# Weight splits of three experts issued in other phases of the expert loop

## The chip, the cores and the metric

The kernel runs on one core of one Trainium2 chip. The metric is the device time of one execution in microseconds (us), as the median of repeated runs. The core has five engines with a queue of instructions each: TensorE (PE, with its weight loads shown as PEld), VectorE (DVE), ScalarE (ACT), GpSimd (POOL) and SyncE (SP), which here issues most of the transfers between memory and the core's own storage.

## The reference, cut to what matters

Chunked attention gives 1536 tokens of 512 features. A gate sends each token to one of eight experts (two matrices, 512x1024 and 1024x512, with a ReLU between them); then a dense layer pair follows for all tokens (512x2048 and 2048x512).

```python
expert_idx = np.argmax(x @ w_gate, axis=1)          # one of E = 8 experts
h = np.maximum(np.einsum('ecd,edf->ecf', disp, w1), 0.0)
y = np.einsum('ecf,efd->ecd', h, w2)
out[i] = gate_w[i] * y[expert_idx[i], pos[i]]       # kept tokens
...
h = x @ w_in
g = np.maximum(0.01 * h, h)
return g @ w_out
```

## The kernel before

Every matrix product is made as three products of a high and a low part, so each operand is first **split**: ACT casts it to the short format (the high part), and DVE subtracts that from the original (the low part). For the weights this is done in **pieces**. A piece is a load of 128x1024 numbers (512 KB) into a buffer named `raw` (five of them) or `more` (three), the cast on line 225 and the subtraction on line 229, both into one of eight slots of a ring (`ring`, each a tile of 128x2x4x512). An expert has four such tiles, A0, B0, A1 and B1 (halves of the first matrix are A, of the second B), and two pieces for each: eight pieces. For the tiles B1 of experts 5 to 7 GpSimd subtracts, in two halves, instead of DVE. When a piece is done, SP issues the next load into the buffer it leaves (line 189), so that up to eight loads are on their way.

An expert (`expert`, lines 751 to 849) runs in six phases. Phases 0 to 3 each make one hidden tile: TensorE multiplies (line 772, `h`), then ACT (lines 823 and 824) and DVE (line 825) write the ReLU's high and low part, `hs`. The rows of the second product (line 779, `acc`) are made in phases 2 to 5. If an expert has 128 tokens or fewer, TensorE takes a shorter form (lines 784, 789, 793), and without tokens it runs filling matmuls (line 798). If it has more than 256 tokens, an overflow block comes ahead of the phases (`block`, lines 851 to 907): transposes (858), the split of the tokens by ACT and DVE (860, 861, `xc`), then its products (874, 892) and its output copies (904, 905). In this trace experts 1, 2, 3 and 7 take the long form, 0, 5 and 6 the short one, 4 has no tokens, and 2, 3 and 7 have the block. Phases 0 and 2 also prepare the next expert's tokens (transposes on line 735, split on 737 and 738, `xsT`). After phase 5 the two output tiles are copied, one by ACT and one by DVE (line 846, `o`), and stored to memory (line 849, `ys`). The slots named `o` are two, and the block's output uses them too.

The order on every engine is the order in which the program is written; each engine works through its own queue in that order, and waits on semaphores for the others. What sets the place of the weight pieces is the table `FEED`: after the instructions of phase `ph` of expert `e`, the generator `weights_gen` is stepped `FEED[e][ph]` times, and each step issues one piece (or nothing, when no slot of the ring is free). `RETIRE` says in which phase an expert's tile gives its slot back:

```python
RETIRE = (None, ("A", 0), None, ("A", 1), ("B", 0), ("B", 1))
...
            self.retired |= {RETIRE[ph] and (RETIRE[ph][0], e, RETIRE[ph][1])}
...
            self.feed(FEED[e][ph])
        if e + 1 < E:
            self.enter(e + 1)
        o = [self.npool.tile([P, DM], F32, name="o", tag="o", bufs=2) for _ in range(2)]
        for j in range(2):
            (nc.scalar.copy if j else nc.vector.tensor_copy)(out=o[j], in_=y[j])
```

`enter` issues whatever pieces of the next expert are still missing; with both tables nothing is missing there. The pieces run ahead of the experts: those issued during expert 1 belong to experts 2 and 3, those issued during expert 3 to experts 4 and 5.

Of the kernel before, what the change touches and what calls it, by code (L numbers as in the profile page):

```python
# [38 lines left out]
DRAIN_FEED = ((0, 0), (1, 0), (1, 0), (0, 0))  # L39
ROUTE_STEPS = 5  # L40
ROUTE_FEED = ((15, 0), (19, 0), (20, 0))
FEED = ((2, 0, 0, 3, 2, 1), (3, 0, 0, 3, 3, 2), (3, 0, 0, 3, 3, 2), (2, 0, 0, 3, 3, 1),
        (2, 0, 0, 3, 2, 1), (2, 0, 0, 3, 2, 1), (2, 0, 0, 1, 1, 0), (1, 1, 1, 1, 0, 0))
AHEAD = ((0, (0, 1)), (0, (2, 3)), (None, ()), (1, (0, 1)), (1, (2,)), (1, (3,)))
RETIRE = (None, ("A", 0), None, ("A", 1), ("B", 0), ("B", 1))
# [8 lines left out]
class Builder:  # L54
# [696 lines left out]
    def expert(self, e):  # L751
# [54 lines left out]
        for ph, (many, few) in enumerate(phases):  # L806
# [32 lines left out]
            else:  # L839
                self.ahead(ph)  # L840
            self.feed(FEED[e][ph])
        if e + 1 < E:
# [216 lines left out]
```

## Time and profile before

| | us |
|---|---|
| median of three runs | 596.9 (596.17 to 598.88) |
| the profiled execution | 594.74 |
| its span, first to last instruction | 593.0 |
| TensorE busy (share of the span) | 533.7 (90%) |
| DVE busy | 402.5 (68%) |
| ACT busy | 298.6 (50%) |
| GpSimd busy | 119.6 (20%) |
| mean granted TensorE clock | 0.969 of full speed |

A row of the timeline gives the start and the busy time of a few like instructions in a row, the engine, the line, the operation with the tiles it writes and reads, their number, and in brackets how long the engine had been idle before and for whom it waited. An engine named "DVEq" is its sequencer, here at a branch. The expert stage runs from about 91 to 311 us of the span, the dense layers from there to the end.

### The profile page before, as it was taken

What the parts mean: (1) busy time and instruction counts of PE and PEld (TensorE: products, weight loads), DVE (VectorE), ACT (ScalarE), POOL (GpSimd) and SP (SyncE); (2) the same over time, 40 slices, a digit from 0 to 9 for tenths busy, and PEclk for the clock granted to TensorE, in tenths of its full rate; (3) what the DMA queues carried; (4) which work ended last, traced back from release to release, by engine and by line L of the source; (5) the groups of instructions that cost most, each with busy time, mean ns of one, the idle gap of its engine ahead of it and who ended that gap; (6) DMA issues with size and microseconds to landing.
All of it is one profiled execution on the core that took longest, in us unless ns stands there. A gap on an engine that the chain in (4) does not pass through costs nothing.

```text
span 593.0 us, 9379 instructions
## 1 busy us (share of the span) xinstructions
PE 533.7 (90%) x3338; PEld 432.0 (73%) x3338; DVE 402.5 (68%) x680; ACT 298.6 (50%) x520; POOL 119.6 (20%) x144
## 2 busy tenths in 40 slices
PE   7799957997997997899998999998999999999995
PEld 5566635795986975677976878877878788778884
DVE  5776776877175357672787877868888788882442
ACT  7999735846173357861544464543443444422220
POOL 7333235028320015633202000000000000000222
PEclk8999976999997999899999999999999999999999
DMA  8998959998769439975343212212113111000111
GB/s 194 199 200 197 243 192 278 389 329 195 162 202 332 135 103 329 329 230 161 108 131 120 75 68 71 72 55 88 49 59 83 35 60 37 0 1 0 72 71 71
DMA packets 66378, 84.85 MB, mean 143 GB/s; under 512 B 23168, under 2 KB 39568, under 8 KB 66320
## 3 DMA queue, kind: packets, MB, share of 16 engines
q1 hardware_dynamic: 60016, 66.46, 38.5%
q0 software_dynamic: 5296, 15.77, 8.8%
q10 hardware_dynamic: 1008, 1.84, 0.8%
q8 instruction: 38, 0.62, 0.4%
q14 instruction: 20, 0.16, 0.1%
HBM read 70.66 MB, written 13.39 MB: 142 GB/s over the span
## 4 chain that ended last, share of the span: by engine, by line
DVE 30%; PE 11%; issue 8%; ACT 7%; POOL 2%; DMA 1%; POOLq 0%; ACTq 0%; DVEq 0%
DVE t L952 4%; PE acc L965 4%; DVE gt L954 4%; ACT gt L953 4%; DVE c L139 3%; DVE c L142 3%; DVE c L135 3%; DVE ring L122 3%; PE h L945 3%; DVE c L141 2%; DVE c L137 2%; DVE total L979 2%; POOL out_dram L981 2%; DVE c L143 1%; ACT ring L225 1%
## 5 line engine op out<-in xcount | busy, mean ns | idle before, releaser
L965 PE MATMUL acc<-ring,gt 128*128 128x512 f32 x576 | 140.7, 394 | 11.0 <-DVE total L979 4.3
L945 PE MATMUL h<-x,ring 128*128 128x512 f32 x576 | 138.8, 390 | 1.1 <-ACT x L701 1.1
L965 PEld LDWEIGHTS acc<-ring,gt 128*128 128x128 f32 x576 | 108.5, 190 | 37.4 <-ACT t L951 6.8
L945 PEld LDWEIGHTS h<-x,ring 128*128 128x128 f32 x576 | 107.7, 188 | 23.7 <-ACT x L701 1.5
L953 ACT CAST gt<-t 128x512 fp32r<-128x512 f32 x48 | 29.8, 621 | 110.4 <-DVE t L952 110.4
L981 POOL DMA_INDIRECT out_dram<-total,srt x8 | 8.3, 1039 | 249.3 <-DVE total L979 248.1
L954 DVE TENSOR_TENSOR gt<-t,gt 128x512 fp32r<-128x512 f32 x48 | 33.3, 694 | 33.0 <-ACT gt L953 33.0
L951 ACT COPY t<-h 128x512 f32<-128x512 f32 x48 | 28.1, 585 | 49.8 <-PE h L945 45.7
L952 DVE SCALAR_TENSOR_TENSOR t<-h,t 128x512 f32<-128x512 f32 x48 | 32.9, 684 | 30.0 <-ACT t L951 30.0
L772 PE MATMUL h<-xsT,ring 128*128 128x256 f32 x384 | 48.8, 284 | 0.7 <-DVE ring L229 0.7
L825 DVE SCALAR_TENSOR_TENSOR hs<-h,hs 128x512 fp32r<-128x512 f32 x32 | 21.7, 687 | 39.9 <-ACT hs L824 39.9
L772 PEld LDWEIGHTS h<-xsT,ring 128*128 128x128 f32 x384 | 47.1, 191 | 1.4 <-ACT ring L225 1.1
L779 PE MATMUL acc<-ring,hs 128*128 128x512 f32 x192 | 45.6, 391 | 0.0
L229 DVE TENSOR_TENSOR ring<-raw,ring 128x1024 fp32r<-128x1024 f32 x37 | 43.2, 1219 | 2.4 <-ACT ring L225 1.9
L225 ACT CAST ring<-raw 128x1024 fp32r<-128x1024 f32 x43 | 42.6, 1057 | 0.7 <-DMA raw<-in_moe_w_dram 0.7
L779 PEld LDWEIGHTS acc<-ring,hs 128*128 128x128 f32 x192 | 35.3, 188 | 7.0
L640 POOL DMA_INDIRECT nat<-xs,tab x24 | 27.5, 1145 | 54.2 <-PE tp L735 32.8
L824 ACT ACTIVATE hs<-h 128x512 fp32r<-128x512 f32 x32 | 18.9, 606 | 24.9 <-PE acc L779 23.9
L874 PE MATMUL h<-ring,xc 128*128 128x512 f32 x72 | 21.1, 446 | 8.7 <-ACT xc L860 7.8
L229 DVE TENSOR_TENSOR ring<-more,ring 128x1024 fp32r<-128x1024 f32 x21 | 24.6, 1222 | 0.8 <-ACT ring L225 0.5
L874 PEld LDWEIGHTS h<-ring,xc 128*128 128x128 f32 x72 | 14.9, 215 | 13.1 <-ACT xc L860 8.5
L784 PE MATMUL h<-ring,xsT 128*128 128x512 f32 x72 | 21.7, 458 | 3.1 <-DMA nat<-xs,tab 1.5
(184 smaller groups left out, 823.0 us busy)
## 6 DMA issues: line engine op xcount, KB each, us to landing
raw<-in_moe_w_dram SPq DMA_DIRECT2D x43, 512.0 KB, 7.0
more<-in_moe_w_dram SPq DMA_DIRECT2D x21, 512.0 KB, 7.0
raw<-in_moe_w_in_dram SPq DMA_DIRECT2D x16, 512.0 KB, 4.1
raw<-in_moe_w_out_dram SPq DMA_DIRECT2D x16, 512.0 KB, 3.3
kn<-in_k_dram SPq DMA_DIRECT2D x16, 192.0 KB, 2.8
qn<-in_q_dram SPq DMA_DIRECT2D x16, 192.0 KB, 4.6
xs<-x POOLq DMA_DIRECT2D x16, 192.0 KB, 4.6
ys<-o SPq DMA_DIRECT2D x12, 256.0 KB, 9.3
```

What stands on the lines that cost most here:

```text
L225: self.nc.scalar.copy(out=hi, in_=raw)
L229: eng.tensor_tensor(out=lo[:, j:j + n], in0=raw[:, j:j + n], in1=hi[:, j:j + n].bitcast(F32), op=ALU.subtract)
L640: self.nc.gpsimd.indirect_dma_start(out=t, out_offset=None, in_=src, in_offset=bass.IndirectOffsetOnAxis(ap=idx[:, col:col + 1], axis=0))
L772: nc.tensor.matmul(hps[f // 2][:, f % 2 * 256:f % 2 * 256 + 256], w["A", f // 4][:, wi, k, c], xs[xi][:, k, :], start=(n == 0), stop=(n == ...
L779: nc.tensor.matmul(y[j], hs[f // 2][:, hi, c:c + P], w["B", f // 4][:, wi, f % 4, :], start=(f == 0 and n == 0), stop=(f == 7 and n == 2))
L874: nc.tensor.matmul(hp[i], xc[:, xi, k, :], w[:, wi, k, :], start=(n == 0), stop=(n == 11))
L945: nc.tensor.matmul(hps[s], w[:, wi, k, c], X[g][:, xi, k, :], start=(n == 0), stop=(n == 11))
L951: nc.scalar.copy(out=t, in_=hp)
L952: nc.vector.scalar_tensor_tensor(out=t, in0=hp, scalar=0.01, in1=t, op0=ALU.mult, op1=ALU.max)
L953: nc.scalar.copy(out=gt[:, 0, :], in_=t)
L954: nc.vector.tensor_tensor(out=gt[:, 1, :], in0=t, in1=gt[:, 0, :].bitcast(F32), op=ALU.subtract)
L965: nc.tensor.matmul(acc[g][i], gt[s][:, hi, i * P:(i + 1) * P], ws[s][:, wi, s[2], :], start=(s[2] == 0 and n == 0), stop=(s[2] == HQ - 1 a ...
```

## The change

Three rows of the table are changed: for experts 1, 2 and 3 the pieces are issued in other phases. In experts 1 and 2 their sum stays at 11. In expert 3 it goes from 9 to 8; one step of expert 4's phase 0, which found no free slot before, issues the piece that is left, so that from expert 4's phase 1 on both kernels have issued the same pieces. The slots of the ring that the tiles get are others; sizes, formats and the work itself are the same.

```diff
-FEED = ((2, 0, 0, 3, 2, 1), (3, 0, 0, 3, 3, 2), (3, 0, 0, 3, 3, 2), (2, 0, 0, 3, 3, 1),
+FEED = ((2, 0, 0, 3, 2, 1), (4, 2, 0, 3, 2, 0), (5, 2, 0, 2, 2, 0), (2, 2, 0, 2, 2, 0),
         (2, 0, 0, 3, 2, 1), (2, 0, 0, 3, 2, 1), (2, 0, 0, 1, 1, 0), (1, 1, 1, 1, 0, 0))
```

ACT's queue in expert 1, from the next expert's second group of tokens in phase 2 to the output copy, in the kernel before:

```order
L737 CAST xsT_2219<-tp 128x512
L809 UNCONDITIONAL_BRANCH
L824 ACTIVATE hs<-h 128x512
L225 CAST ring<-raw 128x1024 x3
L809 UNCONDITIONAL_BRANCH
L225 CAST ring<-raw 128x1024 x2
L225 CAST ring<-more 128x1024 x2
L809 UNCONDITIONAL_BRANCH
L225 CAST ring<-more 128x1024
L846 COPY o<-acc 128x512
```

and in the changed one:

```order
L737 CAST xsT_2219<-tp 128x512
L824 ACTIVATE hs<-h 128x512
L225 CAST ring<-raw 128x1024 x2
L225 CAST ring<-more 128x1024 x2
L809 UNCONDITIONAL_BRANCH
L225 CAST ring<-more 128x1024
L809 UNCONDITIONAL_BRANCH
L846 COPY o<-acc 128x512
```

Between the last hidden tile (`hs`) and the copy stand five casts instead of eight; the other three now stand in phases 0 and 1, where three stood before. DVE's subtractions (line 229) moved with them. Expert 2 has the same pattern, with four instead of eight.

DVE's queue in expert 3, from the last hidden tile to the branch of the next expert's block, before:

```order
L825 SCALAR_TENSOR_TENSOR hs<-h,hs 128x512
L229 TENSOR_TENSOR ring<-more,ring 128x1024 x3
L229 TENSOR_TENSOR ring<-raw,ring 128x1024
L809 UNCONDITIONAL_BRANCH
L229 TENSOR_TENSOR ring<-raw,ring 128x1024 x2
L809 UNCONDITIONAL_BRANCH
L846 COPY o<-acc 128x512
L762 COMPARE_AND_BRANCH
```

and after:

```order
L825 SCALAR_TENSOR_TENSOR hs<-h,hs 128x512
L229 TENSOR_TENSOR ring<-more,ring 128x1024
L229 TENSOR_TENSOR ring<-raw,ring 128x1024
L809 UNCONDITIONAL_BRANCH
L229 TENSOR_TENSOR ring<-raw,ring 128x1024 x2
L809 UNCONDITIONAL_BRANCH
L846 COPY o<-acc 128x512
L762 COMPARE_AND_BRANCH
```

Two of the six subtractions left this place; they stand behind the second hidden tile of the same expert now.

GpSimd's queue from the end of expert 3 to the gathers of tokens for expert 6, before (the branch on line 762 is the start of expert 4):

```order
L809 UNCONDITIONAL_BRANCH x3
L229 TENSOR_TENSOR ring<-raw,ring 128x512 x2
L762 UNCONDITIONAL_BRANCH
L809 UNCONDITIONAL_BRANCH
L229 TENSOR_TENSOR ring<-raw,ring 128x512 x2
L640 DMA nat<-xs,tab 128x512
```

and after:

```order
L809 UNCONDITIONAL_BRANCH x2
L762 UNCONDITIONAL_BRANCH
L809 UNCONDITIONAL_BRANCH
L229 TENSOR_TENSOR ring<-raw,ring 128x512 x4
L640 DMA nat<-xs,tab 128x512
L809 UNCONDITIONAL_BRANCH x2
```

The two halves of one piece moved from the end of expert 3 into expert 4, so that four stand in a row ahead of the gathers.

## Rows read from the trace of the kernel before

**Rows 1.** The page, busy time, share of the span and instructions of each engine.

```profile
PE 533.7 (90%) x3338; PEld 432.0 (73%) x3338; DVE 402.5 (68%) x680; ACT 298.6 (50%) x520; POOL 119.6 (20%) x144
```

**Rows 2.** Stretches: length, busy time by engine, granted clock, DMA share, GB/s.

```profile
138.00:141.50 3.50, 0.38 (x3) 0.17 (x2) 3.50 (x4) 3.50 (x6) 2.89 (x3) 1.00 0.94 326
...
178.00:181.50 3.50, 0.43 (x4) 0.19 (x2) 3.50 (x4) 3.50 (x6) 0.94 (x1) 0.85 0.87 294
181.50:188.00 6.50, 6.45 (x17) 5.06 (x18) 3.49 (x5) 0.66 (x2) 0.00 (x0) 0.55 0.92 313
...
220.50:232.00 11.50, 9.06 (x39) 6.39 (x39) 8.04 (x11) 8.93 (x15) 8.66 (x7) 1.00 1.00 342
```

**Rows 3.** Timeline, end of expert 1 and start of expert 2's block.

```profile
132.85 4.84 ACT L225 CAST ring<-raw 128x1024 fp32r<-128x1024 f32 x5
...
133.93 5.77 DVE L229 TENSOR_TENSOR ring<-raw,ring 128x1024 fp32r<-128x1024 f32 x5 [0.25 <-ACT ring L225]
...
137.58 2.94 ACT L225 CAST ring<-more 128x1024 fp32r<-128x1024 f32 x3
...
139.61 3.49 DVE L229 TENSOR_TENSOR ring<-more,ring 128x1024 fp32r<-128x1024 f32 x3
140.42 0.58 ACT L846 COPY o<-acc 128x512 f32<-128x512 f32 x1
...
140.90 0.65 ACT L860 CAST xc<-tp 128x256 fp32r<-128x256 f32 x2
...
141.33 2.11 PE L874 MATMUL h<-ring,xc 128*128 128x512 f32 x8 [3.12 <-ACT xc L860]
...
144.35 2.81 PE L874 MATMUL h<-ring,xc 128*128 128x512 f32 x11 [0.92 <-DVE xc L861]
```

**Rows 4.** Timeline, end of expert 2 and start of expert 3's block.

```profile
173.08 1.99 ACT L225 CAST ring<-raw 128x1024 fp32r<-128x1024 f32 x2
...
181.55 7.29 PE L874 MATMUL h<-ring,xc 128*128 128x512 f32 x19 [3.12 <-ACT xc L860]
```

**Rows 5.** Timeline, start of expert 7's block.

```profile
268.18 4.65 PE L874 MATMUL h<-ring,xc 128*128 128x512 f32 x19 [1.57 <-ACT xc L860]
```

**Rows 6.** Timeline, end of expert 3 to expert 5; last but one: landing of 230.07's gather.

```profile
219.26 3.49 DVE L229 TENSOR_TENSOR ring<-raw,ring 128x1024 fp32r<-128x1024 f32 x3
...
223.66 0.63 PE L735 MATMUL tp<-ident,nat 128*128 128x128 f32 x4 [1.50 <-DVEq L762]
...
226.11 2.54 POOL L229 TENSOR_TENSOR ring<-raw,ring 128x512 fp32r<-128x512 f32 x2 [1.00 <-ACT ring L225]
...
230.07 0.95 POOL L640 DMA_INDIRECT nat<-xs,tab  x1 [0.30 <-issue]
...
DMA to landing us min/median/max: 6.1/6.1/6.1
...
238.58 1.09 PE L735 MATMUL tp<-ident,nat 128*128 128x128 f32 x4 [3.32 <-DVEq L762]
```

**Rows 7.** Timeline, first half of expert 1; last: the page's median landing of loads.

```profile
111.72 4.91 SPq L189 DMA_DIRECT2D raw<-in_moe_w_dram x5
...
126.37 0.60 ACT L824 ACTIVATE hs<-h 128x512 fp32r<-128x512 f32 x1 [3.69 <-PE acc L779]
...
raw<-in_moe_w_dram SPq DMA_DIRECT2D x43, 512.0 KB, 7.0
```

**Rows 8.** Timeline, expert 2; last: landing of expert 1's output store, issued at 143.6.

```profile
154.54 3.04 PE L772 MATMUL h<-xsT,ring 128*128 128x256 f32 x24
...
160.32 0.37 ACT L904 COPY o<-acc 128x256 f32<-128x256 f32 x1 [9.52 <-DMA ys<-o]
...
163.59 2.90 PE L779 MATMUL acc<-ring,hs 128*128 128x512 f32 x12
...
169.63 8.36 PE L779 MATMUL acc<-ring,hs 128*128 128x512 f32 x36
...
DMA to landing us min/median/max: 16.6/16.6/16.6
```

## The prediction

> **What bounds the kernel now.** I read the page first, then the stretches, then the timeline from the first expert to the last. Over the whole span TensorE is busy for 533.7 of 593.0 us, DVE for 402.5 and ACT for 298.6 [rows 1], so TensorE is the bound and what counts is where it stands still between 114 and 252 us, the experts 1 to 5. The stretches show two places where it hardly works while ACT and DVE have no free moment: 138.0 to 141.5 (TensorE 0.38 of 3.50 us, ACT and DVE 3.50 each) and 178.0 to 181.5 (0.43 of 3.50) [rows 2]. They are the ends of experts 1 and 2. The timeline shows why. After the last hidden tile of expert 1, ACT casts eight weight pieces without a pause, five from 132.85 and three from 137.58, and DVE subtracts eight behind it, until 143.10; only then come the output copies (L846) and the casts of the next expert's overflow block (L860, L861), for which TensorE waits 3.12 us, and then 0.92 us more for the low half [rows 3]. Expert 2 ends in the same way, again eight pieces: ACT has no pause from 178.0 to 181.5 [rows 2], TensorE waits 3.12 us, and what it does then goes at half speed: nineteen matmuls take 7.29 us [rows 4], where the same nineteen take 4.65 us in expert 7's block [rows 5]. At the end of expert 3, TensorE waits 1.50 us for DVE, which has six pieces, the last three until 222.75, and the output copy in front of the skipped block's branch [rows 6].
>
> So the splits are not too much work for ACT and DVE; they stand in the wrong place, ahead of the few short instructions for which TensorE waits at an expert's end.
>
> **The change part by part.** The number of pieces split in experts 1 and 2 stays at eleven each. What moves is their place: in expert 1 six instead of three before the last hidden tile, in expert 2 seven instead of three, in expert 3 four instead of two. Behind the last hidden tile stand five, four and four, instead of eight, eight and seven. Expert 3 passes one piece (for GpSimd) on to expert 4, where a call that did nothing stood before.
>
> End of expert 1. Five casts take 4.84 us, from 132.85 to 137.69. TensorE's last matmul ends at 141.33 - 3.12 = 138.21, and that is the block's transposes; its rows end some 0.5 earlier. So ACT is free when the accumulator is: copy at about 137.8, cast 0.48 later, first matmul 0.43 after that, at 138.75 instead of 141.33 [rows 3]. DVE ends its fifth piece at 133.93 + 5.77 = 139.70. From the end of its last piece (139.61 + 3.49 = 143.10) to TensorE's second start (144.35) it needs 1.25 now, so the low half is there at 140.95. The eight matmuls before it, 2.11 us, end at 140.9. The second start moves from 144.35 to 140.95 or a little later: I take **-3.3 us**. Bounds: -2.6 (what ACT's shorter queue gives, 141.33 to 138.75, and no more) and -4.04 (both waits gone entirely).
>
> End of expert 2. Two casts from 173.08 end at 175.07; the next two write a slot that this expert's own rows read until then, so they may start 0.3 late and end at about 177.4, before TensorE's transposes end at 181.55 - 3.12 = 178.43. By the same steps as above the block starts at 178.9 to 179.1: **-2.5 us**, between -2.0 and -3.1.
>
> The clock. From 181.5 to 188.0 the granted clock is 0.55 on average, and it was 0.85 in the stretch with the wait before [rows 2]; 0.5 is 1.2 GHz, the lower of its two levels. TensorE had stood still for 3.12 us before that. With 0.5 us of standing still I expect 2.4 GHz throughout, as in the stretch from 138.0, and 4.65 us for the nineteen: 7.29 - 4.65 = **-2.6 us**, between 0 and -2.6. The Trainium skill (TensorE: Matmul & The Clock Gate, the section on the HAM clock gate) says that the watch over TensorE's activity runs on its own time and doesn't start with the kernel, so that the place of a transition varies between runs. This trace agrees as far as it goes: a wait of 3.12 us left the clock at 1.00 after expert 1 and halved it after expert 2. By that rule the fall could be absent in the timed runs, or come elsewhere; that is a rival below.
>
> End of expert 3. DVE's three pieces from 219.26 end at 222.75, and TensorE starts 0.91 later, at 223.66 [rows 6]. With two pieces fewer (2 x 1.16) that is 221.3, and TensorE, itself busy until 223.66 - 1.50 = 222.16, no longer waits: -1.5. In expert 4 ACT has one cast more, some 0.97 us [rows 3], ahead of the hidden tiles; part of it fills idle time there, and I let 0.4 of the 1.5 go. GpSimd now does two pieces in a row there, 2.54 us each (one of them ended at 226.11 + 2.54 = 228.65 before, both end at about 230.0 after), and behind them stand the gathers for expert 6. The second of them moves from 230.07 to 231.4. It landed 6.1 us after its issue; by that it lands at 237.5, just when TensorE will want it (238.58 - 1.1) [rows 6]. I take another 0.3 off for that: **-0.8 us**, between -1.5 and +1.3 (a gather whose issue and landing take 2.4 us longer).
>
> What the moved pieces could cost at the front. In expert 1 ACT is idle for 3.69 us before the third hidden tile at 126.37 [rows 7]. Three more casts at 0.97 fit: 2.9 of 3.69. DVE has three more too, 3.5 us, of which some 0.7 push its next tile back, and TensorE wants that tile several us later. The data: the loads of the three moved pieces are the first three of five issued between 111.72 and 116.63, and a load lands in a median of 7.0 us [rows 7]; the casts would want them at about 121.7, 123.7 and 124.7, some 10 us after their issue. In expert 2 five pieces stand ahead of the second hidden tile instead of three. TensorE's first 24 matmuls end at 157.58 now [rows 8], 154.3 after; with some 3 us for the first tile and the next expert's columns and 5.8 for five pieces, DVE has the second tile ready at about 164. TensorE wants it behind the rows of the first, at 169.63 now [rows 8], 166.3 after. I take 0. If the cover were gone, a piece is 0.97 on ACT and 1.16 on DVE.
>
> Sum: 3.3 + 2.5 + 2.6 + 0.8 = 9.2 us. The profiled execution took 594.74 us, 593.0 of it span; it becomes 585.5. The median of the runs is 596.9, 2.2 above that, and I take the sum from it as well: **587.7 us**. Everything behind expert 5 keeps its order, and the long last stage starts earlier by as much.
>
> **The rivals.**
> (a) The clock gives nothing: it falls elsewhere, or the timed runs never had that fall. For it speaks that equal waits had unequal results; against it that no other wait of 3 us is left up to 235 us. Then the sum is 6.6: 590.3.
> (b) The gain is waited away in experts 4 to 6, because loads set the pace there: from 220.5 to 232.0 the DMA engines are at a share of 1.00 and move 342 GB/s [rows 2]. Against it: splits there wait for DVE and ACT, not for loads, and the loads now leave earlier. Then the time is within 3 us of 596.9.
> (c) Slower. Expert 1's output must land in memory before ACT may copy expert 2's block: ACT stood for 9.52 us until 160.32 for that, the store having taken 16.6 us, and TensorE took the first hidden tile 3.3 us after, without standing [rows 8]. With the block 3.3 earlier TensorE wants that tile at 160.3, so the store has to land by 157.0. It leaves 3.4 us earlier than at 143.6, since DVE is done at 139.70 instead of 143.10, and behind five loads instead of eight; even at 16.6 us it lands at 156.8. From there each us late is a us of TensorE, and the two extra pieces ahead of the second hidden tile add up to 2.3. To eat 9.2 us and 3 more it would have to land 9.9 late, 26.5 us after its issue: 600. The Trainium skill (DMA: Bandwidth & Descriptors, the section on queues, rings and completion order) says that on each DMA engine the descriptors of one ring are consumed in order and rings of different issuers take turns. By that a store behind five loads lands sooner than one behind eight, which is for the forecast; no run here shows it for five.
> (d) More than forecast: the wait of 3.32 us before 238.58 comes from DVE's six pieces in expert 4, which the change leaves alone. The clock falls there too: the four transposes behind it take 1.09 us, those at 223.66 only 0.63 [rows 6]. If the wait becomes a little shorter, that fall may go as well: 0.5 us there and about as much in the matmuls behind, so 586.5.
>
> **How the numbers follow.** Forecast 0.64, (a) 0.16, (b) 0.08, (c) 0.04, (d) 0.08. Half a per cent, 3.0 us, is about what a measurement of this kernel can tell from no change. Forecast, (a) and (d) are faster by more: 0.88. (b) is within: 0.08. (c) is slower: 0.04. The terms at their upper ends give 4.04 + 3.1 + 2.6 + 1.5 = 11.2, or 585.7, and 1 less with (d), with some room for the runs' own spread: I go to 584.0. At (a) with the gathers late by 1.3 instead of 0.8 early it is 592.4: I go to 592.5. That leaves out (b) and (c) and tails, under 2 in 10.
>
> **What would show it.** Right: TensorE's first L874 of experts 2 and 3 waits under 1 us; the nineteen matmuls of expert 3 take about 4.65 us with the granted clock at 1.00; L735 at expert 4's start has no wait for DVE; five, four and four casts stand between the last hidden tile and L846; ACT never waits for a load in the fronts. Wrong: a wait of TensorE for a hidden tile (L824, L825) inside experts 1 to 3, a wait for the gathered rows at expert 5's L735 well over 3.3 us, or a distance from expert 5's start to the end that grows by as much as its start came forward.

## The result, and the profile after

The changed kernel takes 589.6 us (median of four runs, 588.7 to 590.4), where the kernel before took 597.2 beside it. The ratio is 0.988, with a 95% interval of 0.985 to 0.990: 7.2 us faster, between 5.7 and 8.7. The forecast was 587.7, in a range of 584.0 to 592.5. The profiled execution took 588.73 us instead of 594.74, 6.0 less. The page of the changed kernel, its span and the first row [rows 1]:

```profile
span 586.9 us, 9376 instructions
...
PE 532.0 (91%) x3338; PEld 430.6 (73%) x3338; DVE 403.2 (69%) x680; ACT 298.9 (51%) x520; POOL 120.3 (20%) x144
```

The work is the same, 3338 matmuls; that TensorE is busy for 1.7 us less goes with its higher clock (0.977 of full speed on average, for 0.969). The waits are what changed. TensorE's waits in the kernel before, by line and what it waited for (us in total, times, the longest):

```profile
PE h L874 <- ACT xc L860: 7.8, 3, 3.1
PE tp L735 <- DVEq L762: 4.8, 2, 3.3
PE tp L735 <- DMA nat<-xs,tab: 2.0, 1, 2.0
```

and in the changed one:

```profile
PE tp L735 <- DMA nat<-xs,tab: 10.1, 4, 3.8
...
PE h L874 <- ACT xc L860: 2.7, 3, 1.6
```

The waits at the blocks went from 7.8 to 2.7 us, those for DVE's branch are gone, and waits for gathered rows went from 2.0 to 10.1. Of these 10.1, 3.1 stand in expert 0, ahead of everything that the change moves; the other 6.9 are new, at expert 5's start. So there is a large gain and a loss that eats part of it, and they have different places. The timeline of the changed kernel at the ends of experts 1 and 2 [rows 3, 4]:

```profile
133.04 1.99 ACT L225 CAST ring<-raw 128x1024 fp32r<-128x1024 f32 x2
...
134.93 2.95 ACT L225 CAST ring<-more 128x1024 fp32r<-128x1024 f32 x3
...
136.39 3.49 DVE L229 TENSOR_TENSOR ring<-more,ring 128x1024 fp32r<-128x1024 f32 x3
...
138.04 0.58 ACT L846 COPY o<-acc 128x512 f32<-128x512 f32 x1 [0.16 <-issue]
...
138.96 4.98 PE L874 MATMUL h<-ring,xc 128*128 128x512 f32 x19 [0.56 <-ACT xc L860]
...
175.73 4.61 PE L874 MATMUL h<-ring,xc 128*128 128x512 f32 x19 [0.52 <-ACT xc L860]
```

Five casts instead of eight stand ahead of the copy, and TensorE waits 0.56 us, once, instead of 3.12 and 0.92. The nineteen matmuls of expert 2's block end at 138.96 + 4.98 = 143.94, those of before at 144.35 + 2.81 = 147.16: 3.2 us earlier. Those of expert 3's block end at 180.34 instead of 188.84: 8.5 earlier. Here is the stretch with expert 3's nineteen (length, busy time by engine, granted clock, DMA share, GB/s), and one in expert 5:

```profile
175.70:180.10 4.40, 4.37 (x19) 3.63 (x20) 1.49 (x3) 0.63 (x2) 0.73 (x1) 1.00 1.04 357
232.90:237.20 4.30, 4.30 (x15) 3.44 (x14) 0.69 (x1) 2.48 (x3) 2.21 (x2) 0.64 1.03 379
```

The first ran at 1.00 where it was 0.55 before [rows 2]; the second is the fall of the clock behind the new wait. The timeline there, experts 4 and 5 [rows 6]:

```profile
213.47 0.60 PE L735 MATMUL tp<-ident,nat 128*128 128x128 f32 x4
...
216.31 5.05 POOL L229 TENSOR_TENSOR ring<-raw,ring 128x512 fp32r<-128x512 f32 x4 [15.09 <-ACT ring L225]
...
220.66 4.04 DVE L229 TENSOR_TENSOR ring<-more,ring 128x1024 fp32r<-128x1024 f32 x3
221.50 1.78 POOL L640 DMA_INDIRECT nat<-xs,tab  x1
...
223.59 1.94 POOL L640 DMA_INDIRECT nat<-xs,tab  x1 [0.30 <-DVE ring L229]
...
228.89 0.60 ACT L823 ACTIVATE t<-h 128x512 f32<-128x512 f32 x1 [3.05 <-DVEq L762]
...
229.03 0.32 PE L735 MATMUL tp<-ident,nat 128*128 128x128 f32 x1 [3.83 <-DMA nat<-xs,tab]
...
232.44 0.90 PE L735 MATMUL tp<-ident,nat 128*128 128x128 f32 x3 [3.09 <-DMA nat<-xs,tab]
```

At expert 4's start there is no wait for DVE: L735 runs at 213.47 instead of 223.66, 10.2 us earlier. At expert 5's start L735 waits for expert 6's rows, twice; the last transposes end at 233.34, where they ended at 239.67 before: 6.3 earlier. DVE's branch, for which TensorE waited until 238.58 before, let ACT go at 228.89 now. So 3.9 of 10.2 us are lost in one place, to two gathers. The first of the two waits ends at nearly the same time as this branch (229.03 and 228.89) and belongs to the branch more than to the gathers: row3_late_piece below waits 3.33 us there for DVE alone. Most of the loss is the second, 3.09.

### The profile page after: what moved, and what is told of

Same layout as the page of the kernel before. It is cut to its first block, busy times and chain, and to the rows that moved or that the text cites. A ratio compares the mean times of both kernels' runs of the same rounds, so it can differ in the third digit from the quotient of the medians.

```text
span 586.9 us, 9376 instructions
## 1 busy us (share of the span) xinstructions
PE 532.0 (91%) x3338; PEld 430.6 (73%) x3338; DVE 403.2 (69%) x680; ACT 298.9 (51%) x520; POOL 120.3 (20%) x144
## 4 chain that ended last, share of the span: by engine, by line
PE 34%; DVE 33%; ACT 12%; issue 11%; DMA 4%; POOL 3%; SPq 1%; ACTq 0%; POOLq 0%; DVEq 0%
PE h L772 6%; PE acc L779 5%; DVE t L952 4%; PE acc L965 4%; DVE gt L954 4%; ACT gt L953 4%; DVE c L142 3%; DVE c L139 3%; DMA nat<-xs,tab 3%; PE h L874 3%; DVE c L135 3%; PE acc L892 3%; PE h L945 3%; DVE ring L122 3%; DVE c L137 2%
## 5 line engine op out<-in xcount | busy, mean ns | idle before, releaser
L965 PE MATMUL acc<-ring,gt 128*128 128x512 f32 x576 | 140.6, 394 | 11.3 <-DVE total L979 4.3
L640 POOL DMA_INDIRECT nat<-xs,tab x24 | 30.3, 1263 | 50.6 <-PE tp L735 35.7
L784 PE MATMUL h<-ring,xsT 128*128 128x512 f32 x72 | 20.9, 447 | 3.1 <-DMA nat<-xs,tab 1.5
L142 DVE TENSOR_TENSOR c<-raw,c 128x512 f32<-128x512 f32 x32 | 22.2, 694 | 1.2
L139 DVE SCALAR_TENSOR_TENSOR c<-c 128x512 uint32<-128x512 uint32 x32 | 22.2, 694 | 1.1
```

The lines of the kernel that those rows point to most:

```text
L139: dv.scalar_tensor_tensor(out=c[1], in0=c[0], scalar=0xC0000000, in1=c[1], op0=ALU.bitwise_and, op1=ALU.bitwise_or)
L142: dv.tensor_tensor(out=cf[0], in0=lo_f, in1=cf[0], op=ALU.mult)
L640: self.nc.gpsimd.indirect_dma_start(out=t, out_offset=None, in_=src, in_offset=bass.IndirectOffsetOnAxis(ap=idx[:, col:col + 1], axis=0))
L965: nc.tensor.matmul(acc[g][i], gt[s][:, hi, i * P:(i + 1) * P], ws[s][:, wi, s[2], :], start=(s[2] == 0 and n == 0), stop=(s[2] == HQ - 1 a ...
```

## The experiments

Eleven runs in three groups, each beside runs of the kernel before on its chip. All change the table, and some a line or two more; edits are given against the changed kernel, rows of the table by their index. Since the time ahead of expert 2 differs by up to 1.5 us between executions, TensorE's place in them is compared from one point: the start of the transposes of expert 2's block (L858), up to which all the kernels are alike on TensorE. The table gives the start of four later instructions in the profiled executions, counted from there, less the same in the kernel before (40.23, 82.93, 101.72 and 128.41 us); minus is earlier. The last column is the ratio of the timed runs, with its 95% interval.

| kernel | block of 3 (L858) | fills of 4 (L798) | second step of 5 (L784) | block of 7 (L858) | ratio |
|---|---|---|---|---|---|
| changed | -3.4 | -8.7 | -6.5 | -6.5 | 0.988 (0.985 to 0.990) |
| changed_again | -3.4 | -8.7 | -6.6 | -6.0 | 0.988 (0.985 to 0.991) |
| row1_only | -3.4 | -4.6 | -4.7 | -4.6 | 0.992 (0.990 to 0.993) |
| row2_only | +1.6 | -3.7 | -3.9 | -3.3 | 0.992 (0.989 to 0.994) |
| row3_only | +2.0 | +2.2 | +4.5 | +4.9 | 1.006 (1.003 to 1.009) |
| row3_undone | -3.4 | -8.6 | -8.7 | -8.6 | 0.988 (0.986 to 0.991) |
| row3_undone_again | -3.4 | -8.7 | -8.8 | -8.5 | 0.982 (0.979 to 0.985) |
| row3_late_piece | -3.4 | -8.6 | -10.6 | -9.7 | 0.981 (0.979 to 0.983) |
| row3_late_piece_again | -3.4 | -8.7 | -10.8 | -10.7 | 0.984 (0.981 to 0.987) |
| gathers_early | -3.4 | -8.7 | -9.8 | -8.6 | 0.984 (0.982 to 0.986) |
| row4_too | -3.0 | -8.3 | -10.1 | -9.7 | 0.981 (0.978 to 0.984) |
| late_piece_a61_on_gpsimd | -3.4 | -8.6 | -11.9 | -11.5 | 0.980 (0.977 to 0.982) |

The changed kernel once more (changed_again) was expected at 588.4, with its runs within 2 us of each other if the order of the instructions sets the loss, and 2 to 4 us apart if it hangs on how the rows meet the loads. It took 589.4, and its six runs lay 2.0 us apart, which is on the border and tells nothing.

The two theories for the loss at expert 5: the gathers are late because expert 3's row puts a GpSimd piece ahead of them and moves them beside DVE's subtractions (a matter of order); or the DMA engines are full there, and the rows are late because the whole stage came 8.5 us earlier.

**Expert 3's row undone** (row3_undone and row3_undone_again).

```diff
- FEED[3] = (2, 2, 0, 2, 2, 0)
+ FEED[3] = (2, 0, 0, 3, 3, 1)
```

> Expert 3 feeds as before, experts 1 and 2 as changed. Theory (the passed-on GpSimd piece holds expert 6's gathers back): TensorE keeps -8.5 us up to the end of expert 3, waits 1.5 us for DVE again at expert 4's start, and finds the gathered rows landed at expert 5's start, where it waits about 3.3 us for DVE's branch only. The span is 8.5 us under the kernel before, 2.4 us under the changed one: about 587.2 where the changed one has 589.6. Rival (loads fill the DMA engines there, so the rows land late whoever issues them): the wait for the rows at expert 5's start stays at 6 us or more, and the time is within 0.7 us of 589.6.

> Expert 3's row undone, once more: six runs lay at two places, 585.7 to 587.0 and 589.5 to 591.4. Theory: the lower place is the kernel without the loss at expert 5, 2.4 us under the changed one; the upper is some other wait of about 4 us that comes in some runs, between experts 1 and 6; if the profiled run falls on the upper place, its timeline shows a wait that the first one didn't have. Rival: the spread is the chip's, not the kernel's; then all runs here lie within 2 us.

The timeline of row3_undone:

```profile
219.52 0.97 POOL L640 DMA_INDIRECT nat<-xs,tab  x1 [0.15 <-DMA raw<-in_moe_w_dram]
...
220.79 0.95 POOL L640 DMA_INDIRECT nat<-xs,tab  x1 [0.30 <-issue]
221.48 3.50 DVE L229 TENSOR_TENSOR ring<-more,ring 128x1024 fp32r<-128x1024 f32 x3 [0.24 <-ACT ring L225]
...
229.30 0.82 PE L735 MATMUL tp<-ident,nat 128*128 128x128 f32 x4 [3.26 <-DVEq L762]
```

Against the kernel before, everything moved by 8.5 to 9 us and nothing else: 0.97 and 0.95 us for the first two gathers, no wait for rows, 3.26 for DVE's branch, and TensorE keeps its 8.7 us through expert 5. That the stage came 8.5 us earlier falls as the cause, since it came just as much earlier here. That the row's own loads crowd the gathers is not excluded by this run; row3_late_piece and gathers_early below, which keep the row's early pieces, speak against it. In time: the second set lay within 585.3 and 586.7, 3.2 us under the changed kernel beside it, for an expected 2.4. The first set (588.2 in the median, for an expected 587.2) lay at two places, 585.7 to 587.0 and 589.5 to 591.4, three runs each, and its ratio alone doesn't tell it from the changed kernel. Both profiled executions were of the lower place, so what the upper one is stays open.

**Each row alone.**

```diff
row1_only   FEED[1] as changed; FEED[2], FEED[3] as before
row2_only   FEED[2] as changed; FEED[1], FEED[3] as before
row3_only   FEED[3] as changed; FEED[1], FEED[2] as before
```

> Only expert 3's row is changed; experts 1 and 2 feed as in the kernel before. Theory (this row loses by itself, whatever came before it): TensorE reaches expert 4's second step 1.7 us earlier, then waits 3.8 and 3.1 us for expert 6's rows at expert 5's start, with four GpSimd halves in front of the gathers and 1.8 to 1.9 us for each gather's issue: by -1.7 + 3.8 it is 2.1 us slower than the kernel before, between 1 and 3 slower. Rival (the rows came late in the changed kernel only because the whole stage came 8.5 us earlier): 1.5 us faster.

> Only expert 1's row is changed. Theory (terms are independent): expert 2's block starts 3.2 us earlier, as in the changed kernel; expert 2's end keeps its wait of 3.12 us, and the nineteen matmuls of expert 3 their half clock, 7.29 us; the rest as before: -3.2, 593.9 where the kernel before has 597.2. Rival (the fall of the clock belongs to a moment of its own, not to this wait): the nineteen take 4.65 us, or the fall comes elsewhere, and the sum is up to 5.9. Second rival (a gain ahead of loads is waited away in experts 3 to 6): within 0.7 us of 597.2.

> Only expert 2's row is changed. Theory (the wait and the half clock belong together): expert 2's block keeps both its waits (3.12 and 0.92 us), expert 3's starts with 0.5 us of waiting instead of 3.12, and its nineteen matmuls take 4.6 instead of 7.29 us: -2.5 and -2.7 make -5.2, 0.9913 of the kernel before, 591.3 where that has 596.5. Rival, from row1_only, where the wait of 3.13 us was still there and the nineteen took 6.03: the fall is not tied to this wait but moves; then it may come behind expert 1's waits instead, or anywhere, and the gain is between 2.5 and 5.2.

Expert 3's row alone makes the kernel slower, by 0.6% or 3.7 us for an expected 2.1, with an interval that leaves out zero. Of the 4.9 us in its trace 2.0 come ahead of expert 3's block and are not the row's: 0.4 are a lower clock behind expert 1's wait, and some 1.5 a cast for which ACT stood still for 3.48 us (the first row below; the profile calls its releaser remote, and no other run here has such a wait). Between expert 4's start and expert 5's second step it loses 2.3, as the changed kernel does (from -8.7 to -6.5). The timeline of row3_only:

```profile
153.27 0.59 ACT L885 CAST ht<-tp 128x512 fp32r<-128x512 f32 x1 [3.48 <-remote]
...
227.25 5.04 POOL L229 TENSOR_TENSOR ring<-raw,ring 128x512 fp32r<-128x512 f32 x4 [15.18 <-ACT ring L225]
...
232.42 1.79 POOL L640 DMA_INDIRECT nat<-xs,tab  x1
...
234.51 1.95 POOL L640 DMA_INDIRECT nat<-xs,tab  x1 [0.31 <-issue]
...
240.09 0.30 PE L735 MATMUL tp<-ident,nat 128*128 128x128 f32 x1 [4.32 <-DMA nat<-xs,tab]
...
243.45 0.90 PE L735 MATMUL tp<-ident,nat 128*128 128x128 f32 x3 [3.07 <-DMA nat<-xs,tab]
```

From 227.25 on it is the same picture, with nothing moved ahead of it. So the loss belongs to this row, whatever precedes it.

Rows 1 and 2 alone each gain 5 us (0.84% and 0.85%); 3.2 were expected of the first, 5.2 of the second. The three together, -0.84 - 0.85 + 0.62 = -1.07%, agree with the changed kernel's -1.2% within the intervals. What they show of the clock is not so simple. The blocks of experts 2 and 3 in row2_only, whose first one has the wait of the kernel before and whose second has the short one:

```profile
141.37 7.43 PE L874 MATMUL h<-ring,xc 128*128 128x512 f32 x19 [3.12 <-ACT xc L860]
...
180.61 4.61 PE L874 MATMUL h<-ring,xc 128*128 128x512 f32 x19 [0.52 <-ACT xc L860]
```

and in row1_only, where expert 3's has the long wait, and expert 5 its wait for DVE:

```profile
177.81 6.03 PE L874 MATMUL h<-ring,xc 128*128 128x512 f32 x19 [3.13 <-ACT xc L860]
...
233.65 0.63 PE L735 MATMUL tp<-ident,nat 128*128 128x128 f32 x4 [3.26 <-DVEq L762]
234.27 3.03 PE L784 MATMUL h<-ring,xsT 128*128 128x512 f32 x12
```

Behind expert 1's wait the clock fell in row2_only, and in the kernel before it didn't, though the code up to there is the same on TensorE and the wait is 3.12 us in both. Behind expert 2's, all nineteen were slow before (7.29), and only part of them in row1_only (6.03). Behind 3.26 us in expert 5 it stayed up. So row1_only's theory was wrong in part (6.03 was neither 7.29 nor 4.65), and the rival right in part: waits of 3 us cost between nothing and 2.7 us of clock, from one execution to the next. Behind the waits of 0.5 us it stayed up in every profile here: the nineteen took 4.97 to 5.01 us in expert 2's block and 4.61 to 4.65 in expert 3's.

**The late piece put back** (row3_late_piece and row3_late_piece_again): the early pieces of expert 3 stay, the piece for GpSimd is issued in its phase 5 again.

```diff
- FEED[3] = (2, 2, 0, 2, 2, 0)
+ FEED[3] = (2, 2, 0, 2, 2, 1)
```

> As the changed kernel, but the piece passed on to expert 4 is issued in expert 3's phase 5 again (row 2, 2, 0, 2, 2, 1). Theory: no wait for DVE at expert 4's start (-10.0 us there, as in the changed kernel), GpSimd has one piece instead of two ahead of the gathers, they are issued at about 219 instead of 221.5 us, and expert 5 waits 3.3 us for DVE only: the span is 9.5 to 10 us under before, 3.5 to 4 us under the changed one, 585.9. Rival (DMA engines full): rows land late all the same, within 0.7 us of 589.6.

> The row 2, 2, 0, 2, 2, 1 for expert 3 once more, beside the other two: 0.981 of the kernel before, within 0.979 and 0.983, since nothing in it hangs on the chip that was drawn; 3 to 4 us under the changed kernel's 0.988.

```profile
212.94 2.55 POOL L229 TENSOR_TENSOR ring<-raw,ring 128x512 fp32r<-128x512 f32 x2 [11.11 <-ACT ring L225]
...
214.16 0.60 PE L735 MATMUL tp<-ident,nat 128*128 128x128 f32 x4
...
219.68 0.96 POOL L640 DMA_INDIRECT nat<-xs,tab  x1
...
220.94 0.95 POOL L640 DMA_INDIRECT nat<-xs,tab  x1 [0.30 <-DMA raw<-in_moe_w_dram]
220.96 1.24 DVE L229 TENSOR_TENSOR ring<-more,ring 128x1024 fp32r<-128x1024 f32 x1 [0.24 <-ACT ring L225]
...
228.79 1.08 PE L735 MATMUL tp<-ident,nat 128*128 128x128 f32 x4 [3.33 <-DVEq L762]
```

This timeline of the first set has what the row was good for and not what it cost: no wait for DVE at expert 4's start (214.16), and gathers of 0.96 and 0.95 us from 219.68 on. TensorE is 10.6 us ahead in expert 5, 584.8 us are 3.6 under what the changed kernel's 0.988 makes of the kernel before there (588.4). The second set came out at 584.6, with one of its six runs at 589.4; its ratio, 0.984, lies above the range named, and its interval overlaps that of the changed kernel. In the traces one digit, the last of the row, is worth the whole loss, 4.1 to 4.3 us at expert 5's second step; by the ratios it is worth 2.4 to 4.2.

**The gathers moved instead of the piece** (gathers_early). `gathers` takes a second argument here, which of the three gathers to issue; its lines are left out.

```diff
+                if ph == 0 and e == 4:
+                    self.gathers(e + 2, (0, 2))
                 if ph == 3 and e + 2 < E:
-                    self.gathers(e + 2)
+                    self.gathers(e + 2, (2, 3) if e == 4 else (0, 3))
```

> The changed kernel, with expert 6's first two gathers issued in expert 4's phase 0 ahead of the two GpSimd pieces instead of in phase 3 behind them. Theory: issued at about 214 us, when DVE doesn't subtract, each takes 0.95 us as before instead of 1.8 to 1.9; the rows land by 222; expert 5's two waits for rows (3.83 and 3.09 us) become one of some 3.7 us for DVE's branch at about 229; the transposes end 3.4 us earlier: 586.2. If the clock also stays up in the twelve matmuls behind (2.98 instead of 4.41 us), 584.8. Rival (the loads that the earlier start moved are what is late there): 589.6 within 0.7, the wait passing on to a cast that waits for its load.

The line numbers behind 715 are up to 3 higher here.

```profile
201.02 0.95 POOL L640 DMA_INDIRECT nat<-xs,tab  x1 [0.30 <-issue]
211.03 1.26 POOL L640 DMA_INDIRECT nat<-xs,tab  x1 [9.06 <-PEq L763]
...
221.38 0.86 PE L799 MATMUL acc<-ring 128*128 128x512 f32 x3 [1.52 <-issue]
...
228.51 0.82 PE L736 MATMUL tp<-ident,nat 128*128 128x128 f32 x4 [2.62 <-DVEq L763]
```

The two waits for rows became one of 2.62 us for DVE, and the time 586.7, for an expected 586.2. Both gathers went earlier than the 214 us expected: GpSimd issued the first at 201.02, right behind expert 5's last, in 0.95 us, and the second at 211.03, in 1.26. TensorE waited for no rows and no cast for its load, so the rival falls as it was put. A gap of 1.52 us inside the filling matmuls, which no other run here has, took back part of the gain; its cause stays open.

**Expert 4's row in the same manner** (row4_too).

```diff
- FEED[3], FEED[4] = (2, 2, 0, 2, 2, 0), (2, 0, 0, 3, 2, 1)
+ FEED[3], FEED[4] = (2, 2, 0, 2, 2, 1), (1, 2, 0, 2, 2, 0)
```

> Expert 3's late piece as in row3_late_piece (row 2, 2, 0, 2, 2, 1), and expert 4's row in the same manner: 1, 2, 0, 2, 2, 0 instead of 2, 0, 0, 3, 2, 1, so that four pieces instead of six stand behind expert 4's last hidden tile on DVE. Theory: TensorE's wait of 3.33 us for DVE's branch at expert 5's start shrinks by two subtractions, 2 x 1.16 = 2.3 us, and the half clock behind it goes (4.14 to 3.0 us): 1.5 to 3.4 us under row3_late_piece, 581.4 to 583.3 by this chip's earlier runs. Rival (the DMA engines are full from 216 to 226 us, and casts in expert 4's phase 1 wait for their loads): within 0.7 us of 584.8, or slower.

```profile
218.47 2.88 DVE L229 TENSOR_TENSOR ring<-more,ring 128x1024 fp32r<-128x1024 f32 x2 [0.25 <-ACT ring L225]
...
219.29 1.77 POOL L640 DMA_INDIRECT nat<-xs,tab  x1 [0.15 <-issue]
...
221.36 0.95 POOL L640 DMA_INDIRECT nat<-xs,tab  x1 [0.30 <-DVE ring L229]
...
223.30 2.97 PE L784 MATMUL h<-ring,xsT 128*128 128x512 f32 x12 [1.87 <-DVE hs L825]
...
228.60 0.63 PE L735 MATMUL tp<-ident,nat 128*128 128x128 f32 x4 [2.33 <-DVEq L762]
```

No gain: 585.2, and 0.981 as row3_late_piece had in its first set. No cast waited for a load, so the rival's reason was wrong, though its time was right. The wait for DVE shrank from 3.33 to 2.33 us, and the one ahead of it grew from 0.69 to 1.87, so that their sum stayed, 4.20 for 4.02; the clock fell all the same (4.59 us for the twelve behind). Expert 4 has no tokens, and TensorE only fills; from 217.5 us on DVE works with hardly a free moment up to the branch, and to put two of its pieces into an earlier phase only moved the wait.

**A tile moved from DVE to GpSimd** (late_piece_a61_on_gpsimd): row3_late_piece, with expert 6's A1 subtracted by GpSimd.

```diff
-OTHERS = (5, 6, 7)
+ONPOOL = {("B", 5, 1), ("B", 6, 1), ("B", 7, 1), ("A", 6, 1)}
...
-            mode = 2 if e in OTHERS and (kind, i) == ("B", 1) else self.share[count % len(self.share)]
+            mode = 2 if (kind, e, i) in ONPOOL else self.share[count % len(self.share)]
```

> row3_late_piece, with expert 6's tile A1 (two pieces, the last of expert 4's queue) subtracted by GpSimd too. It prices the wait of 3.33 us at expert 5's start: DVE has four pieces instead of six there, GpSimd four halves behind the gathers (about 224 to 229.5 us). Theory: the wait shrinks by up to 2 x 1.16 = 2.3 us, and the half clock behind it (4.14 for the twelve against 3.0) may go: 1.5 to 3.4 under row3_late_piece, 0.975 to 0.9785 of the kernel before. Rival (DVE and GpSimd slow each other while both subtract, as 2.54 us became 3.53 before expert 4, and the buffers come back later to the loads): within 0.7 us of row3_late_piece.

```profile
223.97 10.63 POOL L229 TENSOR_TENSOR ring<-raw,ring 128x512 fp32r<-128x512 f32 x8 [0.61 <-ACT ring L225]
...
225.71 0.30 PE L735 MATMUL tp<-ident,nat 128*128 128x128 f32 x1 [1.08 <-DVEq L762]
...
226.91 0.55 PE L735 MATMUL tp<-ident,nat 128*128 128x128 f32 x3 [0.90 <-DMA nat<-xs,tab]
227.42 3.03 PE L784 MATMUL h<-ring,xsT 128*128 128x512 f32 x12
```

Taking work off DVE did shorten the wait, from 3.33 to 1.08 + 0.90 us, and the twelve behind it ran at full clock. TensorE is 11.9 us ahead there and 11.5 at expert 7. Timed, 583.3 us and 0.980 are the best of all, 12 below the kernel before beside it (595.3); the ratio lies above the 0.975 to 0.9785 that was expected. Beside row3_late_piece_again in the same group it is 1.3 us less, for an expected 1.5 to 3.4, and the intervals don't tell the two apart.

## Why the prediction was right, point by point, and which term was not

**End of expert 1**, -3.3: measured -3.2 (143.94 for 147.16), or -3.4 from the common point of the table. ACT's copy came at 138.04 (137.8 worked out), the first matmul at 138.96 (138.75), DVE's last piece ended at 139.88 (139.70). The rule that made it work: from the end of the last piece on, the chain of short instructions keeps its length.

**End of expert 2**, -2.5: measured 3.12 - 0.52 = -2.6.

**The clock**, -2.6: 7.29 - 4.61 = 2.7 in the profiled executions. Rival (a), that it gives nothing, fell there. But the rule that the prediction weighed, from the Trainium skill (TensorE: Matmul & The Clock Gate, the HAM clock gate), holds: the place of a fall varies between executions. Behind expert 1's wait of 3.12 us the granted clock was 1.00 in the kernel before and 0.58 in row2_only. What the change removes is not this one fall but two waits of 3 us, each of which costs up to 2.7 in some executions. That may be why the timed runs gained 7.2 us, and the profiled one 6.0, since the kernel before happened to lose nothing behind expert 1 in its profile; that is an argument and not shown.

**The fronts**, 0: as forecast. ACT's casts in the changed kernel's experts 1 to 3 wait for no load, and TensorE for no hidden tile. Rival (c) didn't come near: L904 of expert 2 went at 154.26, before TensorE wanted it; the store that it waited for, issued at 140.6, took 13.7 us at most, for 16.6. Rival (b) fell with row3_undone: what was gained stays gained through experts 4 to 6.

**End of expert 3**, -0.8, bounds -1.5 to +1.3: this is the term that was mis-sized. It measured -8.5 to -6.3, +2.2, outside its bounds, and row3_only gives it +2.3 in the trace and +3.7 in time. It has two halves. The first, DVE's wait, was right: gone, and ACT's extra cast cost nearly nothing (-10.2 at 213.47 against -10.0 at expert 5's first product, 222.22 for 232.26). The second, the gathers, failed in one step: "It landed 6.1 us after its issue; by that it lands at 237.5". Measured back from expert 3's end (8.5 us added), GpSimd's four halves end at 221.36 + 8.5 = 229.9, as worked out (230.0), and the second gather starts at 232.1, for 231.4. But from start to landing it took not 6.1 but at most 232.44 - 223.59 = 8.85 us. Of these 2.75 us more, 1.0 is its own issue (1.94 for 0.95); the 0.7 by which it started late comes on top, and is the first one's issue (1.78 for 0.97). The remaining 1.75 lie between the end of the issue and the use of the rows, where the DMA share is 0.83 (222 to 229 us) and 0.99 (226 to 234); whether the loads or the order in which rows were fetched made them was not separated.

Why the issue took longer could have been read in the trace before. There the third gather, which no term used, began while DVE was in the middle of a piece, and took 1.48 instead of 0.95. The piece and the gather in the kernel before, and then the piece beside the changed kernel's second gather (223.59, above):

```profile
230.76 1.22 DVE L229 TENSOR_TENSOR ring<-more,ring 128x1024 fp32r<-128x1024 f32 x1 [0.24 <-ACT ring L225]
231.32 1.48 POOL L640 DMA_INDIRECT nat<-xs,tab  x1 [0.31 <-issue]
...
223.50 1.21 DVE L229 TENSOR_TENSOR ring<-more,ring 128x1024 fp32r<-128x1024 f32 x1
```

In the kernel before the piece ends at 231.98 and the gather at 232.80, 0.82 us later; in the changed one they end at 224.71 and 225.53, 0.82 us apart again. So the issue had to wait for the end of the piece that was running when it began. The later place put all three gathers behind running pieces, while the prediction took duration and landing from a gather that began with none running. It also compared the landing with where TensorE had wanted the rows before, less 1.1, and not with where it would want them if the first half of the term came true in full.

**The sum** was right in sign and within the range, with an error of 1.9 us in the median: three terms within 0.1 us in the trace, and the fourth 3 us off, of which the timed runs gave back some. That the time came within 1.9 us is in part luck: the timed runs gained 1.2 us more than the profiled one, and why they did isn't shown.

**Rival (d)**, that the fall of the clock in expert 5 goes too: not in the changed kernel, where the twelve behind the wait took 4.41 us. It went in row1_only, in one of the two sets of row3_late_piece, and with the shorter waits, 1.08 and 0.90, in late_piece_a61_on_gpsimd. Its time has a slip: 0.5 us and about as much again below the forecast is 586.7, not 586.5.

## What to carry to other kernels

When a step moves on a queue, look at what runs on the neighbouring engine at its new time, and take its duration from a row in which that neighbour was busy when the step began; a 0.95 us issue that becomes 1.8 and then 1.9 is a late transfer. Where a table moves several things, price each of its numbers apart: here two rows gain 5 us each, and the third loses about 4 of them in the traces by its last digit. And where an engine never rests in a stage, as DVE in expert 4, moving its work within the stage left the sum of the waits as it was, and taking work off it made it smaller.

## What the runs showed of the hardware

A gather's issue on GpSimd takes 0.94 to 1.02 us when no subtraction of DVE is running as it begins. It takes no longer when one begins together with it or behind it: 0.95 in row3_late_piece at 220.94, with DVE's piece from 220.96. When a piece is running as the gather begins, the gather ends 0.82 us or a little more after that piece, however long the piece still had to go: in gathers_early it took 1.26, in the kernel before 1.48, in the changed one 1.78, 1.94 and 1.97. Of 78 gathers that began so, between 118 and 262 us of the thirteen traces, 77 ended 0.81 to 0.89 us after the end of the piece; one waited for the next piece too, and ended 0.82 us after that. So the doubling is no fixed factor: what is added depends on what is left of the piece in front, 1.14 us of it where the issue took 1.97. The Trainium skill (SBUF — State Buffer, the sections on the two separate sides and on who interferes with whom) describes an exclusive lock between DVE and GpSimd, by which the later one stands still until the other's instruction ends. It counts a DVE instruction with two operands in this storage against a GpSimd instruction that reads there, and names copies in DVE's faster modes as what starves a gather's issue. The traces agree with the standing still until the end; that an ordinary subtraction of two operands does it to a gather's issue is from these rows. In the other direction DVE's three pieces took 4.04 us instead of 3.50 when GpSimd's subtraction reached into them (216.31 to 221.36 over 220.66), and two took 2.88 in row4_too.

A wait of 3.1 to 3.3 us by TensorE left the granted clock at 1.00 in some executions and halved it in others, for all or part of the matmuls behind it: the same nineteen took 4.92 (in two parts, 2.11 and 2.81), 6.03, 6.22, 7.29, 7.38 and 7.43 us, the twelve of expert 5, behind a wait for DVE, between 2.99 and 4.60. A single profile doesn't tell what such a wait costs.
